# Attention and gated MLP on one core: two staging places for the sums of the u weights, their stores at set places of SyncE's order, and four copies one product later

## The chip, the core and the metric

The kernel runs as one program on one core of a Trainium2 chip. The core has a matrix engine (TensorE, PE in the profile; its weight loads are PEld), a vector engine (VectorE, DVE), a scalar engine (ScalarE, ACT), a general engine (GpSimd, POOL) and a sequencer that issues nearly all DMAs (SyncE, SP). The metric is the device time of one execution in microseconds. Before the change it is 650.03 us, the median of 3 runs (650.01 to 650.95).

## What is computed

Eight batches, twelve heads, 448 positions, head size 64; sigmoid attention and behind it a gated MLP with a product over positions:

```python
scores = scale * np.matmul(q, k.transpose(0, 1, 3, 2)) - np.log(S)
attn = 1.0 / (1.0 + np.exp(-scores))
x = np.matmul(attn, v)                      # heads side by side: 448 x 768
h = np.maximum(x @ w_in, 0.0)               # 768 x 1024
u, v = h[..., :512], h[..., 512:]
v_n = (v - mean(v)) / np.sqrt(var(v) + 1e-06)
v_s = np.einsum('ts,bsd->btd', w_spatial, v_n) + b_spatial[None, :, None]
out = (u * v_s) @ w_out                     # 512 x 768
```

All in float32. The kernel gets there by splitting an operand into a high and a low part and adding three matrix products (high by high, low by high, high by low).

## The kernel before

The batches go in four rounds `m` of two. A round has its attention, then the gate (`gate_values`, `spatial`), the u product, and the output product (`outputs`). Two-by-two blocks of the u and of the output product are formed with seven block products instead of eight (Strassen's way, in Winograd's form): for this, sums of operands and sums of weights are needed, called S1 to S4 beside the plain blocks A11, A12, A22. In the first round the u product is done straight (`gated`), and while it and the output product run, GpSimd forms the sums of the u weights that the later rounds use. They go to DRAM (`tu_dram`) and are read back in each later round (`factor_loads`).

**The weight sums** are a Python generator, `u_sums` (L589 to L613). For each of three row blocks `c`: two additions (`wsum`, L598) put high and low parts together, four subtractions (L603) form four sums, and each sum is split again into a high part (a copy, L607) and a low part (a subtraction, L609). Three of the four go to DRAM by a store on SyncE's queue (L613), the fourth stays in place of the weights it came from. There is one staging place, `other`; the second sum is staged in its own place in `w_u_s`, and the fourth is written there once that store has landed. The generator stands still at each `yield`, and each call of `load_weights(1)` moves it to the next. These calls stand all over `outputs` (once after each of many products) and in `pair` (once after each score tile and once after the value products), so the calls decide where in the program a store comes to stand.

**The order of each engine is the order of the program text**: `in_program_order` chains the instructions of every engine. So whatever stands behind a waiting store on SyncE's queue waits too. All DMAs of this part of the program stand on that one queue.

**Attention of a later round** (`attention`) is one generator that starts inside `outputs` of the round before (`between`) and runs on behind it. It goes over six pairs of units `p` (a unit is a batch and two heads). A pair has 36 score products (`psc`, L327), sigmoids on ScalarE (`at`, L335) and 24 value products (`pav`, L361); between the two come the splits of the next pair's inputs on VectorE (`qks` from `raw`, L113 and L114). The loads run ahead: `raw` (keys and queries of a unit, four places), `v` (three places), the weights `w_v` of the gate, one piece per pair (L1023), and at the end `last` (L970), the short key tiles of each pair, in the places of `raw`. Behind the first five pairs come the short scores of three pairs (L315, 24 products of half size on `last`), their value products, the same for the other three pairs, and the sixth pair.

**The output product of the first round**: `px` is formed for three column blocks by A11, copied by ScalarE to `us` (L807), then continued in the same PSUM place by A12, which therefore waits for the copy. Beside it `second_sums(i)` forms and splits the operand sums of the second half of the rows: step i stands behind the copy of block i (L774 to L787; high parts by ScalarE, low parts by `lower`, L738, on VectorE).

Of the kernel before, what the change touches and what calls it, by code (L numbers as in the profile page):

```python
# [35 lines left out]
def attn_gmlp_kernel(  # L36
# [552 lines left out]
    def u_sums():  # L589

        copy, add, sub = nc.gpsimd.tensor_copy, nc.gpsimd.tensor_add, nc.gpsimd.tensor_sub
        half = F // 2
        other = const.tile([P, 2, half], F32R, name="other")
        for c in range(NH):
            vals = []
            for cc in (2 * c, 2 * c + 1):
                val = work.tile([P, 512], F32, tag="wval", name=f"wsum_{cc}", bufs=2)
                add(val, w_u_s[:, cc, 0].bitcast(F32), w_u_s[:, cc, 1].bitcast(F32))  # L598
                vals += [val[:, :half], val[:, half:]]
                yield  # L600
            w11, w12, w21, w22 = vals
            for a, b, to in ((w12, w11, w11), (w12, w22, w12), (w22, w11, w22), (w21, w22, w21)):
                sub(to, a, b)  # L603
                yield
            own = w_u_s[:, 2 * c, :, half:]
            for k, val, stage in ((1, w11, other), (2, w12, own), (0, w22, other), (None, w21, own)):
                copy(stage[:, 0], val)  # L607
                yield
                sub(stage[:, 1], val, stage[:, 0].bitcast(F32))  # L609
                yield  # L610
                if k is not None:
                    yield
                    nc.sync.dma_start(tu_dram[:, k, c], stage.bitcast(F32))  # L613

    def u_step(ps, m, i, operand, name, start):

# [112 lines left out]
    def outputs(m, between):  # L729
# [38 lines left out]
        def second_sums(i):  # L768

            a, b = g1  # L770
            s2 = c_tile(1)[:, 1]
            three, last, two, outer = place(0, 5), place(1, 0), place(1, 1), place(1, 2, 2)
            if i == 0:
                sub(b[:, 0], b[:, 0], a[:, 0])  # L774
                add(s2, b[:, 1], b[:, 0])
                copy(three[:, 0], b[:, 0])
                copy(last[:, 0], b[:, 1])
            elif i == 1:
                add(a[:, 0], s2, a[:, 0])
                sub(a[:, 1], a[:, 1], s2)  # L780
                copy(two[:, 0], s2)
                lower(three[:, 1], b[:, 0], three[:, 0])
                lower(last[:, 1], b[:, 1], last[:, 0])
            else:
                copy(outer[:, 0], a)
                lower(two[:, 1], s2, two[:, 0])
                lower(outer[:, 1], a, outer[:, 0])  # L787
                operands[S3, 1], operands[A22, 1], operands[S2, 1] = map(halves, (three, last, two))
                operands[S1, 1], operands[S4, 1] = (halves(outer[:, :, i]) for i in range(2))

        if m:
            first, second = sums_of[m]
            hooks = ((), (), (second, second), (), (), (second,), (first,), (), (second,))
            work_of = iter([lambda gs=gs: [next(g, None) for g in gs] for gs in hooks])
        else:
            gated(b1, pairs[0])
            first_sums()
            gated(b1, pairs[1])
            work_of = iter([lambda i=i: second_sums(i) for i in range(NE)])

        def sums_work():
            next(work_of, lambda: None)()
# [2 lines left out]
        for i in range(NE):  # L805
            step(px[i], m, i, A11, 11, True)
            copy(us[i][:, 0], px[i])  # L807
            sums_work()
        for i in range(NE):
            step(px[i], m, i, A12, 21, False)  # L810
            copy(c_tile(i)[:, 0], px[i])
            nc.sync.dma_start(out[b0, i], cs[i][:, 0])
            sums_work()
        if m == 0:
            between()
        pwy = [banks(f"pw_{m}_{i}") for i in range(NE)]
        pw, py = ([t[:, j, :S] for t in pwy] for j in range(2))
        for i in range(NE):
            step(pw[i], m, i, S3, 3, True)
            load_weights(1)  # L820
            add(us[i][:, 1], us[i][:, 0], pw[i])
            sums_work()
        for i in range(NE):
            step(pw[i], m, i, A22, 4, False)
            load_weights(1)
        if m:
            between()
        for i in range(NE):
            step(py[i], m, i, S2, 2, True)
            load_weights(1)  # L830
            add(cs[i][:, 1], us[i][:, 0], py[i])
            add(cs[i][:, 1], cs[i][:, 1], pw[i])
            nc.sync.dma_start(out[b1, i], cs[i][:, 1])
        for i in range(NE):
            step(py[i], m, i, S1, 1, False)
            load_weights(1)
            add(us[i][:, 1], us[i][:, 1], py[i])
            nc.sync.dma_start(out[b1, NE + i], us[i][:, 1])
        between()
        for i in range(NE):  # L840
            step(py[i], m, i, S4, 22, False)
            load_weights(1)
            add(us[i][:, 0], us[i][:, 0], py[i])
            nc.sync.dma_start(out[b0, NE + i], us[i][:, 0])
        rest = [t for t in (*tmp, *big) if t not in (*us_tags, *cs_tags)]
        tags = [*taken, *cs_tags, *us_tags, *rest]
        taken.clear()
# [93 lines left out]
    def attention(m):  # L941
# [55 lines left out]
        def pair(p):  # L997
            full, tags = [], []
            for t in (*FIRST, *SECOND):
                full.append((*unit(p), t, attention_scores(*unit(p), t, None, free)))  # L1000
                tags.append(free.pop())
                load_weights(1)
            nc.scalar.copy(mark, full[-1][-1][:1, 0, :1])
            if p + 1 < NHP:
                splits(2 * p + 2, 2 * p + 3)
# [176 lines left out]
```

## Time and profile before

| | us |
|---|---|
| time, median of 3 runs | 650.03 |
| the profiled execution, its own time | 650.33 |
| its span on the core | 648.5 |
| TensorE busy in the span | 640.0 |
| VectorE busy | 444.3 |
| ScalarE busy | 326.6 |
| GpSimd busy | 57.6 |
| mean granted TensorE clock, share of full | 0.997 |

The span is the time from the first to the last instruction of one execution; the profiled execution took 1.8 us more than its span, and 0.30 us more than the median of the three runs. A busy TensorE is one with a matmul in flight. The granted clock is the share of full speed (2.4 GHz) that the chip let TensorE have; 0.50 is the lower level of 1.2 GHz.

### The profile page before, as it was taken

The page shows a single profiled execution, that of the slowest core. Times are in us where ns is not written, and L with a number is a line of the kernel's source. Part 1 is how long each engine was busy: PE and PEld are TensorE (multiplying, and loading weights), DVE is VectorE, ACT ScalarE, POOL GpSimd, SP SyncE. Part 2 cuts the span into 40 slices and gives each one's busy share as a digit, 9 for nine tenths or more (in the row PEclk, how much of TensorE's full clock was granted, in tenths as well). Part 3 has the DMA queues.
Part 4 walks back from the last instruction along what each step waited for, and adds up shares of the span by engine and source line. Part 5 has one row for each costly group of instructions (what it writes and reads, how often), then busy time and mean ns, then how long its engine had stood idle before and what let it go on. Part 6 is the DMA issues. An engine that isn't in the chain of part 4 may idle for free.

```text
span 648.5 us, 9489 instructions
## 1 busy us (share of the span) xinstructions
PE 640.0 (99%) x3734; PEld 488.1 (75%) x3734; DVE 444.3 (69%) x630; ACT 326.6 (50%) x519; POOL 57.6 (9%) x78
## 2 busy tenths in 40 slices
PE   9999999999999899999999999999999999999997
PEld 5555789998755368999975547899996545889997
DVE  6888779996657588445854488735775548864494
ACT  5888384223366448611436674930317655681040
POOL 0000011150638001000000000000000000010000
PEclk9999999999999899999999999999999999999999
DMA  8864732073887600543176830047038690032313
GB/s 307 260 228 147 277 96 65 2 297 129 307 280 218 211 2 1 196 162 156 59 262 232 249 130 1 11 184 286 33 129 283 206 293 22 0 130 104 109 43 127
DMA packets 40748, 101.01 MB, mean 156 GB/s; under 512 B 8448, under 2 KB 22528, under 8 KB 40448
## 3 DMA queue, kind: packets, MB, share of 16 engines
q1 hardware_dynamic: 40704, 100.42, 44.6%
q8 instruction: 29, 0.48, 0.3%
q14 instruction: 15, 0.12, 0.1%
HBM read 80.74 MB, written 19.66 MB: 155 GB/s over the span
## 4 chain that ended last, share of the span: by engine, by line
PE 70%; issue 13%; DVE 9%; DMA 4%; POOL 2%; ACT 1%; SPq 1%; POOLq 0%; DVEq 0%; ACTq 0%
PE pv L380 13%; PE pav L361 12%; PE pw L380 11%; PE psc L327 8%; PE pg L380 8%; PE ux L380 7%; PE uy L380 5%; PE px L380 4%; DMA last<-qk_dram 2%; PE psc L315 1%; DMA tu_dram<-w_u_s 1%; DVE vn L431 1%; DVE wval L149 1%; DVE wval L146 1%; DMA tu_dram<-other 1%
## 5 line engine op out<-in xcount | busy, mean ns | idle before, releaser
L335 ACT ACTIVATE at<-psc,bias_s 128x896 f32<-128x896 f32 x168 | 155.6, 1015 | 106.0 <-PE psc L327 81.8
L361 PE MATMUL pav<-at,v 128*64 128x448 f32 (+1 forms) x624 | 119.1, 543 | 0.0
L380 PE MATMUL pv<-w_v,x_s 128*128 128x512 f32 x504 | 115.5, 390 | 0.0
L380 PEld LDWEIGHTS pv<-w_v,x_s 128*128 128x128 f32 x504 | 94.3, 188 | 22.3 <-issue 2.8
L327 PEld LDWEIGHTS psc<-qks 64*128 64x128 f32 x864 | 79.4, 185 | 21.4 <-issue 13.6
L327 PE MATMUL psc<-qks 64*128 64x448 f32 x864 | 94.2, 367 | 0.0
L361 PEld LDWEIGHTS pav<-at,v 128*64 128x64 f32 (+1 forms) x624 | 40.9, 136 | 66.1 <-issue 46.2
L380 PE MATMUL pg<-w_sp_s,vn 128*128 128x448 f32 x352 | 71.7, 362 | 0.0
L380 PEld LDWEIGHTS pg<-w_sp_s,vn 128*128 128x128 f32 x352 | 66.0, 188 | 4.6
L984 DVE COPY whole<-pav 128x896 f32<-128x896 f32 x15 | 16.4, 1092 | 59.4 <-PE pav L361 55.3
L114 DVE TENSOR_TENSOR qks<-raw,qks 128x848 fp32r<-128x848 f32 (+2 forms) x48 | 51.6, 1082 | 6.4 <-ACT qks L113 5.3
L380 PE MATMUL pw<-x_s,factors 128*128 128x448 f32 x261 | 53.8, 362 | 0.0
L380 PEld LDWEIGHTS pw<-x_s,factors 128*128 128x128 f32 x261 | 48.9, 187 | 3.3
L415 POOL TENSOR_SCALAR rstd<-power 128x2 f32<-128x2 f32 (+1 forms) x16 | 4.0, 249 | 461.9 <-ACT pv L412 461.9
L431 DVE SCALAR_TENSOR_TENSOR vn<-rv,rstd,vn 128x512 fp32r<-128x512 f32 (+1 forms) x32 | 23.3, 748 | 23.5 <-ACT vn L426 23.3
L380 PE MATMUL ux<-x_s,w_u_s 128*128 128x448 f32 x162 | 33.4, 362 | 0.0
L426 ACT ACTIVATE vn<-rv,rstd 128x512 fp32r<-128x512 f32 (+1 forms) x32 | 21.8, 717 | 20.7 <-POOL rstd L416 20.6
L380 PEld LDWEIGHTS ux<-x_s,w_u_s 128*128 128x128 f32 x162 | 30.4, 187 | 2.1
L989 DVE TENSOR_TENSOR whole<-whole,pav 128x896 f32<-128x896 f32 x18 | 18.9, 1084 | 15.4 <-PE pav L361 15.4
L380 PE MATMUL pu<-x_s,w_u_s 128*128 128x448 f32 x144 | 29.1, 362 | 0.0
L380 PEld LDWEIGHTS pu<-x_s,w_u_s 128*128 128x128 f32 x144 | 27.0, 187 | 1.8
L656 ACT CAST x_s<-g 128x896 fp32r<-128x896 f32 x6 | 5.6, 941 | 42.9 <-DVE g L649 42.9
(150 smaller groups left out, 812.5 us busy)
## 6 DMA issues: line engine op xcount, KB each, us to landing
raw<-qk_dram SPq DMA_DIRECT2D x47, 456.0 KB, 5.6
v<-v_dram SPq DMA_DIRECT2D x23, 448.0 KB, 5.2
w_v<-w_v_dram SPq DMA_DIRECT2D x18, 512.0 KB, 5.4
factors<-t_dram SPq DMA_DIRECT2D x12, 768.0 KB, 4.8
last<-qk_dram SPq DMA_DIRECT2D x18, 448.0 KB, 5.2
factors<-tu_dram SPq DMA_DIRECT2D x9, 768.0 KB, 5.8
wraw<-w_in_dram SPq DMA_DIRECT2D x12, 512.0 KB, 6.9
out_dram<-cs SPq DMA_DIRECT2D x24, 224.0 KB, 1.9
```

Of the source, the lines that this page charges most:

```text
L114: nc.vector.tensor_sub(lo, src, hi.bitcast(F32))
L146: nc.vector.scalar_tensor_tensor(l, a, 3, l, op0=ALU.logical_shift_left, op1=ALU.bitwise_or)
L149: nc.vector.scalar_tensor_tensor(l, low, 29, l, op0=ALU.logical_shift_right, op1=ALU.bitwise_or)
L315: nc.tensor.matmul(psc[odd * HALF : (odd + 1) * HALF, j, :S], key[rows], query[rows], start=True, stop=True,)
L327: nc.tensor.matmul(psc[:, j, :S], s[rows, a, k : k + P], s[rows, e, REST:PART], start=i == 0, stop=i == len(TERMS) - 1,)
L335: nc.scalar.activation(at, psc[:, :, :S], AF.Sigmoid, bias=bias_s, scale=QK)
L361: nc.tensor.matmul(pav[heads, odd, :S], vt[rows, heads], at[rows, j], start=start, stop=stop)
L380: nc.tensor.matmul(ps, st, mv, start=start and i == 0, stop=i == len(ops) - 1, skip_group_check=not start)
L426: nc.scalar.mul(hi, rv[rows, i], rstd[rows, i : i + 1])
L431: nc.vector.scalar_tensor_tensor(lo, rv[rows, i], rstd[rows, i : i + 1], hi.bitcast(F32), op0=ALU.mult, op1=ALU.subtract,)
L984: copy(whole, pav)
L989: nc.vector.tensor_add(whole, whole, pav)
```

## The change

`u_sums` has two staging places, `others[0]` and `others[1]`, used in turn. A step `stage(n)` forms and splits one sum; the sum that stays in place is now written first of its row block, straight from the additions, and nothing is staged in `w_u_s`. Each move of the generator issues store `n` and then works on sum `n + 2`. The calls of `load_weights` are taken out of the loops and stand at chosen places: one behind the first product of `outputs`, two behind the second, one behind each of the last three, and two in each `pair` (one behind all score tiles, one behind the value products). `second_sums` has four steps instead of three: its copies and lower parts move one step, that is one product, later.

```diff
-        other = const.tile([P, 2, half], F32R, name="other")
-        for c in range(NH):
...
-            own = w_u_s[:, 2 * c, :, half:]
-            for k, val, stage in ((1, w11, other), (2, w12, own), (0, w22, other), (None, w21, own)):
-                copy(stage[:, 0], val)
-                yield
-                sub(stage[:, 1], val, stage[:, 0].bitcast(F32))
-                yield
-                if k is not None:
-                    yield
-                    nc.sync.dma_start(tu_dram[:, k, c], stage.bitcast(F32))
+        others = [const.tile([P, 2, half], F32R, name=f"other_{i}") for i in range(2)]
+
+        def halved(to, val):
+            copy(to[:, 0], val)
+            sub(to[:, 1], val, to[:, 0].bitcast(F32))
+
+        def stage(n, vals):
+            if n % 3 == 0:
...
+                w11, w12, w21, w22 = vals
+                for a, b, to in ((w12, w11, w11), (w12, w22, w12), (w22, w11, w22), (w21, w22, w21)):
+                    sub(to, a, b)
+                halved(w_u_s[:, 2 * c, :, half:], w21)
+            halved(others[n % 2], vals[(0, 1, 3)[n % 3]])
+
+        vals = []
+        stage(0, vals)
+        stage(1, vals)
+        for n in range(3 * NH):
+            yield
+            nc.sync.dma_start(tu_dram[:, (1, 2, 0)[n % 3], n // 3], others[n % 2].bitcast(F32))
+            if n + 2 < 3 * NH:
+                stage(n + 2, vals)
@@ second_sums(i) in outputs
             if i == 0:
                 sub(b[:, 0], b[:, 0], a[:, 0])
                 add(s2, b[:, 1], b[:, 0])
-                copy(three[:, 0], b[:, 0])
-                copy(last[:, 0], b[:, 1])
             elif i == 1:
                 add(a[:, 0], s2, a[:, 0])
                 sub(a[:, 1], a[:, 1], s2)
+                copy(three[:, 0], b[:, 0])
+                copy(last[:, 0], b[:, 1])
+            elif i == 2:
                 copy(two[:, 0], s2)
+                copy(outer[:, 0], a)
                 lower(three[:, 1], b[:, 0], three[:, 0])
                 lower(last[:, 1], b[:, 1], last[:, 0])
             else:
-                copy(outer[:, 0], a)
                 lower(two[:, 1], s2, two[:, 0])
                 lower(outer[:, 1], a, outer[:, 0])
@@ outputs: calls of load_weights
+        load_weights(1)
         for i in range(NE):
             step(px[i], m, i, A12, 21, False)
             copy(c_tile(i)[:, 0], px[i])
             nc.sync.dma_start(out[b0, i], cs[i][:, 0])
             sums_work()
+        load_weights(2)
...
@@ pair(p) in attention
             for t in (*FIRST, *SECOND):
                 full.append((*unit(p), t, attention_scores(*unit(p), t, None, free)))
                 tags.append(free.pop())
-                load_weights(1)
+            load_weights(1)
```

ScalarE in the first round's output product, before. `x_s` are the high parts of the operand sums, `us` the copies that free the three `px` places for A12:

```order
L759 CAST x_s_76<-g_0_0_1099 128x2x448
L760 CAST x_s_76<-cs_0_0_1355 128x448
L807 COPY us_0_0_1314<-px_0_0_1404 128x448
L776 CAST x_s_76<-g_1_2_1299 128x448
L777 CAST x_s_76<-g_1_2_1299 128x448
L807 COPY us_0_1_1315<-px_0_1_1405 128x448
L781 CAST x_s_76<-cs_0_1_1414 128x448
L807 COPY us_0_2_1316<-px_0_2_1406 128x448
L785 CAST x_s_76<-g_0_2_1139 128x2x448
```

The same stretch of ScalarE after the change:

```order
L766 CAST x_s_76<-g_0_0_1099 128x2x448
L767 CAST x_s_76<-cs_0_0_1355 128x448
L815 COPY us_0_0_1314<-px_0_0_1404 128x448
L815 COPY us_0_1_1315<-px_0_1_1405 128x448
L786 CAST x_s_76<-g_1_2_1299 128x448
L787 CAST x_s_76<-g_1_2_1299 128x448
L815 COPY us_0_2_1316<-px_0_2_1406 128x448
L789 CAST x_s_76<-cs_0_1_1414 128x448
L790 CAST x_s_76<-g_0_2_1139 128x2x448
```

The second `us` copy now stands ahead of the two casts of `g_1_2`, and the third ahead of the cast of `cs_0_1`. VectorE's order is the same before and after.

SyncE's queue from the first loads behind the first round's outputs, before (`raw_3_0` is the unit of batch 3, heads 0 and 1; the stores are those to `tu_dram`; two of nine stand ahead of this stretch):

```order
L271 DMA v_2_4_1611<-v_dram 128x896
L613 DMA tu_dram_82<-other_1478 128x512
L262 DMA raw_3_0_1699<-qk_dram 128x912
L262 DMA raw_3_1_1701<-qk_dram 128x912
L271 DMA v_3_0_1703<-v_dram 128x896
L1023 DMA w_v_1_1606<-w_v_dram_78 128x1024
L613 DMA tu_dram_82<-other_1478 128x512
L262 DMA raw_3_2_1788<-qk_dram 128x912
L262 DMA raw_3_3_1790<-qk_dram 128x912
```

The same stretch after the change, with five stores ahead of it:

```order
L271 DMA v_2_4_1645<-v_dram 128x896
L618 DMA tu_dram_82<-other_1_1440 128x512
L618 DMA tu_dram_82<-other_0_1439 128x512
L262 DMA raw_3_0_1729<-qk_dram 128x912
L262 DMA raw_3_1_1731<-qk_dram 128x912
L271 DMA v_3_0_1733<-v_dram 128x896
L1031 DMA w_v_1_1640<-w_v_dram_78 128x1024
L618 DMA tu_dram_82<-other_1_1440 128x512
L618 DMA tu_dram_82<-other_0_1439 128x512
L262 DMA raw_3_2_1814<-qk_dram 128x912
L262 DMA raw_3_3_1816<-qk_dram 128x912
```

Here stand the sixth to ninth store, all of them ahead of `raw_3_2`, where there were the third and the fourth.

SyncE's queue at the end of the fifth pair, before (`last_2_4` and `last_3_0` are the short key tiles of the third and the fourth pair):

```order
L1023 DMA w_v_1_1606<-w_v_dram_78 128x1024
L613 DMA tu_dram_82<-other_1478 128x512
L613 DMA tu_dram_82<-w_u_s_79 128x2x256
L613 DMA tu_dram_82<-other_1478 128x512
L970 DMA last_2_4_2065<-qk_dram 128x2x64
L970 DMA last_2_4_2065<-qk_dram 128x2x448
L970 DMA last_3_0_2068<-qk_dram 128x2x64
L970 DMA last_3_0_2068<-qk_dram 128x2x448
```

The same place after the change:

```order
L1031 DMA w_v_1_1640<-w_v_dram_78 128x1024
L978 DMA last_2_4_2067<-qk_dram 128x2x64
L978 DMA last_2_4_2067<-qk_dram 128x2x448
L978 DMA last_3_0_2070<-qk_dram 128x2x64
L978 DMA last_3_0_2070<-qk_dram 128x2x448
```

The last three stores, which stood ahead of these loads, are gone from here.

## Rows read from the trace of the kernel before

**Rows 1.** The page's first section: busy time, share and instructions of each engine.

```profile
PE 640.0 (99%) x3734; PEld 488.1 (75%) x3734; DVE 444.3 (69%) x630; ACT 326.6 (50%) x519; POOL 57.6 (9%) x78
```

**Rows 2.** Busy time by stretch: length, then PE, PEld, DVE, ACT, POOL, clock, DMA.

```profile
140.00:150.00 10.00, 9.02 (x45) 8.12 (x44) 9.83 (x14) 5.81 (x11) 1.08 (x2) 1.00 0.87 319
...
210.00:220.00 10.00, 6.86 (x52) 2.58 (x52) 3.17 (x3) 2.91 (x3) 1.57 (x3) 0.84 0.87 272
```

**Rows 3.** Timeline of PE at px: start, us, operation, [idle before, releaser].

```profile
141.60 4.97 PE L380 MATMUL px<-gs,w_out_s 128*128 128x448 f32 x24
147.54 2.68 PE L380 MATMUL px<-gs,w_out_s 128*128 128x448 f32 x12 [0.98 <-ACT us L807]
150.06 14.56 PE L380 MATMUL pw<-x_s,factors 128*128 128x448 f32 x72
```

**Rows 4.** The chain that ended last: the same px products in the second round.

```profile
305.17 7.21 PE px L380 x36
```

**Rows 5.** Timeline of ACT in the stretch of rows 3.

```profile
146.03 0.57 ACT L776 CAST x_s<-g 128x448 fp32r<-128x448 f32 x1 [2.46 <-DVE g L774]
...
146.97 0.52 ACT L807 COPY us<-px 128x448 f32<-128x448 f32 x1
```

**Rows 6.** Timeline of DVE in the same stretch.

```profile
138.77 1.05 DVE L756 TENSOR_TENSOR cs<-g 128x448 f32<-128x448 f32 x1
...
141.57 2.23 DVE L738 TENSOR_TENSOR x_s<-g,x_s 128x896 fp32r<-128x896 f32 x2
...
145.37 0.62 DVE L774 TENSOR_TENSOR g<-g,g 128x448 f32<-128x448 f32 x1
```

**Rows 7.** Timeline of PE: fourth pair, short scores, sixth pair, in the second round's attention.

```profile
193.60 3.88 PE L327 MATMUL psc<-qks 64*128 64x448 f32 x36
...
210.54 1.73 PE L315 MATMUL psc<-last 64*64 64x448 f32 x16
215.42 0.98 PE L315 MATMUL psc<-last 64*64 64x448 f32 x8 [3.14 <-DMA last<-qk_dram]
...
224.99 3.88 PE L327 MATMUL psc<-qks 64*128 64x448 f32 x36
```

**Rows 8.** Timeline of PE: short scores and sixth pair, third and fourth round.

```profile
372.67 2.49 PE L315 MATMUL psc<-last 64*64 64x448 f32 x24
...
382.21 3.88 PE L327 MATMUL psc<-qks 64*128 64x448 f32 x36
...
529.88 2.49 PE L315 MATMUL psc<-last 64*64 64x448 f32 x24
...
539.73 3.88 PE L327 MATMUL psc<-qks 64*128 64x448 f32 x36
```

**Rows 9.** Busy time by stretch, as rows 2, one microsecond behind the wait.

```profile
217.00:218.00 1.00, 1.00 (x11) 0.42 (x7) 0.49 (x1) 0.53 (x1) 0.00 (x0) 0.50 1.07 359
```

**Rows 10.** Timeline of SP in the second round's attention.

```profile
171.33 1.72 SPq L262 DMA_DIRECT2D raw<-qk_dram  x2
...
210.52 0.32 SPq L613 DMA_DIRECT2D tu_dram<-other  x1
210.93 1.96 SPq L970 DMA_DIRECT2D last<-qk_dram  x4
```

**Rows 11.** Timeline of SP in the third round's attention, same loads.

```profile
367.09 2.47 SPq L970 DMA_DIRECT2D last<-qk_dram  x4
```

**Rows 12.** Timeline of POOL: the third store's sum, and the second row block.

```profile
164.99 0.40 POOL L607 CAST other<-wsum 128x256 fp32r<-128x256 f32 x1 [23.82 <-DMA tu_dram<-other]
...
171.75 3.31 POOL L598 TENSOR_TENSOR wsum<-w_u_s 128x512 f32<-128x512 f32 x2
...
181.20 1.41 POOL L609 TENSOR_TENSOR w_u_s<-wsum,w_u_s 128x256 fp32r<-128x256 f32 x1
```

**Rows 13.** DMA issues from 180 to 195 us: size of one, median us to landing.

```profile
raw<-qk_dram SPq DMA_DIRECT2D x4, 456.0 KB, 6.1
```

**Rows 14.** Busy time by stretch, as rows 2; its end is DMA share and GB/s.

```profile
174.00:180.00 6.00, 6.00 (x50) 3.92 (x48) 3.19 (x4) 3.25 (x5) 5.68 (x7) 1.00 0.96 357
```

More of the change, by code (lines that the diff above doesn't have):

```diff
@@ L592, in u_sums @@
         half = F // 2
-        other = const.tile([P, 2, half], F32R, name="other")
-        for c in range(NH):
[L595 to L599, printed above, removed]
-                yield
-            w11, w12, w21, w22 = vals
-            for a, b, to in ((w12, w11, w11), (w12, w22, w12), (w22, w11, w22), (w21, w22, w21)):
-                sub(to, a, b)
-                yield
-            own = w_u_s[:, 2 * c, :, half:]
-            for k, val, stage in ((1, w11, other), (2, w12, own), (0, w22, other), (None, w21, own)):
-                copy(stage[:, 0], val)
-                yield
-                sub(stage[:, 1], val, stage[:, 0].bitcast(F32))
-                yield
-                if k is not None:
-                    yield
-                    nc.sync.dma_start(tu_dram[:, k, c], stage.bitcast(F32))
+        others = [const.tile([P, 2, half], F32R, name=f"other_{i}") for i in range(2)]
[4 more added lines that the diff above has]
+            if n % 3 == 0:
+                c = n // 3
+                vals.clear()
+                for cc in (2 * c, 2 * c + 1):
+                    val = work.tile([P, 512], F32, tag="wval", name=f"wsum_{cc}", bufs=2)
+                    add(val, w_u_s[:, cc, 0].bitcast(F32), w_u_s[:, cc, 1].bitcast(F32))
+                    vals += [val[:, :half], val[:, half:]]
+                w11, w12, w21, w22 = vals
[11 more added lines that the diff above has]
+                stage(n + 2, vals)
     def u_step(ps, m, i, operand, name, start):
@@ L798, in outputs @@
             gated(b1, pairs[1])
-            work_of = iter([lambda i=i: second_sums(i) for i in range(NE)])
+            work_of = iter([lambda i=i: second_sums(i) for i in range(NE + 1)])
         def sums_work():
@@ L833, in outputs @@
             nc.sync.dma_start(out[b1, i], cs[i][:, 1])
+        load_weights(1)
         for i in range(NE):
             step(py[i], m, i, S1, 1, False)
-            load_weights(1)
             add(us[i][:, 1], us[i][:, 1], py[i])
             nc.sync.dma_start(out[b1, NE + i], us[i][:, 1])
+        load_weights(1)
         between()
@@ L841, in outputs @@
             step(py[i], m, i, S4, 22, False)
-            load_weights(1)
             add(us[i][:, 0], us[i][:, 0], py[i])
             nc.sync.dma_start(out[b0, NE + i], us[i][:, 0])
+        load_weights(1)
         rest = [t for t in (*tmp, *big) if t not in (*us_tags, *cs_tags)]
@@ L1001, in pair @@
                 tags.append(free.pop())
-                load_weights(1)
+            load_weights(1)
             nc.scalar.copy(mark, full[-1][-1][:1, 0, :1])
```

2 lines of the change are left out of this document (removed).

## The prediction

> **What bounds the kernel now.** I read the page's busy times first: TensorE is busy for 640.0 of 648.5 us [rows 1], so an edit on another engine is worth only what TensorE now stands idle, or runs slow, because of it. The table by stretch then shows where that is. Two stretches stand out in the part of the program that the diff touches: 140 to 150, with 9.02 us busy of 10, and 210 to 220, with 6.86 of 10 and a mean clock of 0.84 [rows 2]. The timeline of TensorE names the releasers. At 146.6 it waits 0.98 us for a `us` copy of ScalarE [rows 3]. At 212.3 it waits 3.14 us for a `last` load [rows 7]. Behind that second wait the granted clock is 0.50, the 1.2 GHz level [rows 9]; a mean of 0.84 over 10 us makes that about (1 - 0.84) x 10 / 0.5 = 3.2 us long [rows 2]. Around the first wait it stayed at 1.00 [rows 2].
>
> An idle figure leaves out the drain of the products before it and the slow ones behind it, so I price both places by a start-to-start distance against the same work in another round.
>
> First place: 36 `px` products run from 141.60 to 150.06, 8.46 us [rows 3]; in the second round they take 7.21 [rows 4]. It costs 1.25.
>
> Second place: from the start of the short scores to the sixth pair, 224.99 - 210.54 = 14.45 us [rows 7]; in the third round 382.21 - 372.67 = 9.54, in the fourth 539.73 - 529.88 = 9.85 [rows 8]. It costs 4.60 to 4.91, of which 3.14 is the wait and up to 1.77 the lower clock and the refill.
>
> The later rounds run the same loads without any weight sums, so they are what the second round should look like with the stores out of the way.
>
> **The copies, one product later.** Nothing is added or removed; ScalarE's order changes. Before, the second `us` copy stands behind two casts of `g_1_2`, which wait for VectorE's L774 until 146.03; the copy ends at 146.97 + 0.52 = 147.49 and TensorE goes on at 147.54 [rows 3, 5]. Its source, the second `px` block, is complete after 12 products of 0.2 us, at 144.0. After, that copy runs at 144.0 to 144.5, far ahead of its use. The third copy now takes the second's slot and ends at 147.49. It is wanted by the 31st product, at 141.60 + 30 x 0.2 = 147.6, whose weights are loaded one product earlier, 147.4. So the wait does not vanish by a wide margin: what is late next is this third copy, by 0.1 to 0.15. Gain 1.25 - 0.15 = 1.1, if VectorE's chain to L774 stays where it is.
>
> It may not stay. GpSimd's work moves: six operations that split sums (the sum left in `w_u_s`, then both staging places) come where four were before the generator stopped, and they last about 2.5 us longer into this stretch, to some 143.7. VectorE's L756 beside GpSimd took 1.05, where L774 of the same size, with GpSimd standing still, took 0.62 [rows 6]: 0.43 per hit. The two lower parts L738 at 141.57 are newly beside GpSimd. On the other side the first write now waits for the last read of the plain weights by TensorE, which leaves L754 and L756 alone for a while. I take 0.1 net and keep from no hit (gain 1.25) to two hits behind a late copy (1.25 - 0.15 - 0.86 = 0.24). Taken: **1.0**.
>
> The Trainium skill (SBUF — State Buffer, section Who interferes with whom) speaks against this part: it says that a VectorE instruction with two SBUF inputs and a GpSimd instruction that reads SBUF do not share the port, one is blocked for the whole instruction. By that rule a hit would cost up to a GpSimd subtraction, 1.41 us as in [rows 12], the whole gain of the copies would go, and the time would be 645.4; the row's 0.43 is less than that, so here the trace does not bear it out in full, and the sum goes by the row.
>
> Behind `px` nothing waits for the moved lower parts: VectorE's order is unchanged, and the first operand that `pw` needs of them is cast at the same 146.03.
>
> **The stores.** Nine stores, and GpSimd's 42 operations, are the same in number. Before, one staging place and a late first store made GpSimd idle 23.82 us for that store [rows 12], so the sums ran late and the last store was issued at 210.52, with the `last` loads of the third and fourth pair right behind it at 210.93 [rows 10]. In the third round the same loads are issued at 367.09, 5.58 us ahead of the short scores [rows 8, 11]; here they were issued 0.39 us behind their start. After, no store stands there, all four calls in `pair` being used up in the second pair. What bounds these loads next is the split that frees their places and the transfers ahead of them, as in the third and fourth round. That gives 4.91 by the third round and 4.60 by the fourth, which still waited a little for `last`. I take **4.6**, since here the queue has been held up more than in either.
>
> What pays for it is the queue in the first two pairs. The seventh store stands ahead of `raw_3_0` and waits for the first sum of the third row block. GpSimd can begin that block when it has used the landing of the fourth store. The fourth store stands where the second stood before, and the work on that landing ended at 171.75 [rows 12]; 1.0 earlier now, 170.75. The second row block took from 171.75 to 181.20 + 1.41 = 182.61, 10.86 us for the same ten operations [rows 12]. So the seventh store goes at about 181.6 and `raw_3_0` at 182.0, where it went at 171.33 before [rows 10]. At 6.1 us to landing [rows 13] it is there at 188.1. Its products begin at 193.60 - 1.0 = 192.6 [rows 7], and between lie two VectorE operations of at most 1.1 each (L738 of 896 columns: 2.23 for two [rows 6]). TensorE is covered by 2.3 us. The ninth store waits for the seventh to land and one more split, and `raw_3_2` behind it is wanted one pair later, 8.5 us ((210.54 - 193.60) / 2 [rows 7]). So the delay costs nothing by this count; without that cover every microsecond of it would be TensorE's.
>
> VectorE's operations of the last three products read one operand from PSUM. GpSimd's second row block now lies beside them; I bound that by the hit above, 0 to 0.43 each. They only empty PSUM places that TensorE wants again one product of three blocks later, and I take 0.
>
> **The sum.** Profiled execution 650.33 - 1.0 - 4.6 = 644.7. The median of the runs was 0.30 lower: 650.03 - 5.6 = **644.4**. With all terms at their ends: 650.03 - 1.25 - 4.91 = 643.9 to 650.03 - 0.24 - 4.60 = 645.2. Everything behind the sixth pair shifts as a whole, since TensorE is without a pause there.
>
> **Rivals.**
>
> (a) *The gap at the short scores shrinks but stays.* The loads that `raw_3_0` heads are issued 10.7 us late and must catch up. At 357 GB/s, the rate of a stretch with the engines 0.96 busy [rows 14], a load of 456 KB takes 1.3 us. If two of them are still queued when the last `last` loads go, these land 2.6 us late, and the fourth round shows that they have no slack. Then 644.4 + 2.6 = 647.0, and with the lower clock behind it again 648.8. For it: the late queue. Against it: the loads behind have 20 us to catch up in, and DMA stood idle in part of them before. Chance 0.20, spread over 645.2 to 648.7.
>
> The page TensorE: Matmul & The Clock Gate of the Trainium skill (What's actually happening) says that the gate judges on a grid of its own that does not begin with the program. By that rule even a shorter gap could be answered by the lower clock, and 648.8 would be the time of this rival rather than 647.0; the trace has one wait with it and one without [rows 2, 9], which fits but does not decide.
>
> (b) *The gap stays whole*, because the loads are bound by the splits here and not by the stores: only the copies gain, 650.03 - 1.0 = 649.0. Against it: SyncE's rows, with the store 0.4 us ahead of the load [rows 10]. Chance 0.06.
>
> (c) *Slower: the queue blocks the fourth pair.* Place: seventh store, `raw_3_0`. It decides from 192.6 - 2.2 - 6.1 - 0.4 = 183.9: a first sum ready later than that makes TensorE wait as much. To end over 1.3 us slower it must eat 5.6 + 1.3, of which a second fall of the clock would give 1.8, so 5.1 of waiting: a sum at 189.0, 7.4 us later than worked out, for work that took 10.9 before. 650.03 + 1.3 and more, say 652. For it: GpSimd slowed by VectorE, whose splits now fall beside it. Chance 0.06.
>
> (d) *The change does not do what it says for the copies* (VectorE late by more than two hits): 645.4. It lies at the edge of the forecast and is counted with (a).
>
> **How the numbers follow.** Forecast 644.4, 643.9 to 645.2: 0.65. (a) and (d) 0.20, (b) 0.06, (c) 0.06, better than the forecast's ends 0.03. The range 643.7 to 647.2 holds the forecast, most of the better case and two thirds of (a), 0.8. A measurement of this kernel can tell about 0.2%, 1.3 us, from no change. Faster by more than that (under 648.7): forecast, better, and (a), 0.87. Within: (b), and a little of (a) and (c), 0.08. Slower: 0.05.
>
> **What would show it.** Right: 36 `px` products in 7.2 to 7.6 us; short scores to sixth pair in 9.5 to 9.9, with the clock at 1.00; no store to `tu_dram` later than about 190; `raw_3_0` issued near 182 and the fourth pair of the second round still following the third without a pause. Wrong: a wait of TensorE for `raw` or `qks` between 185 and 205, a wait for `last` of more than 0.5 us, or VectorE's L774 later than 146.4.

## The result

The changed kernel took 643.64 us (median of 4 runs, 643.47 to 644.28) against 650.49 for the kernel before (4 runs, 650.01 to 653.01): ratio 0.9889, 95% interval 0.9862 to 0.9916. Two later series, each on one chip with its own runs of before, gave 644.14 against 650.82 (0.9898, 0.9882 to 0.9915) and 643.93 against 650.60 (0.9893, 0.9876 to 0.9911). It is faster by 1.0 to 1.1%, 6.7 to 6.9 us, where 5.6 was forecast. One execution among all that follow ran at a mean granted clock of 0.85 (712 us, in the run called late_block); it is left out.

Both waits of TensorE that the prediction priced are gone. The table by stretch of the changed kernel (length, then busy time of PE, PEld, DVE, ACT, POOL, the granted clock, DMA share and GB/s) answers [rows 2]:

```profile
140.00:150.00 10.00, 10.00 (x51) 9.06 (x50) 9.68 (x13) 7.13 (x13) 4.10 (x4) 1.00 0.76 302
...
210.00:220.00 10.00, 10.00 (x104) 4.14 (x98) 7.90 (x10) 6.98 (x8) 0.00 (x0) 1.00 0.50 177
```

Before, TensorE was busy for 9.02 and 6.86 us in these two stretches. TensorE's timeline in the changed kernel answers [rows 3, 7, 8] (start, us, line, operation; an idle time ahead of a row would stand in brackets):

```profile
140.74 7.61 PE L380 MATMUL px<-gs,w_out_s 128*128 128x448 f32 x36
148.18 14.79 PE L380 MATMUL pw<-x_s,factors 128*128 128x448 f32 x72
162.82 3.77 PE L380 MATMUL pw<-x_s,w_out_s 128*128 128x448 f32 x18
166.51 3.88 PE L327 MATMUL psc<-qks 64*128 64x448 f32 x36
...
208.90 2.49 PE L315 MATMUL psc<-last 64*64 64x448 f32 x24
...
218.44 3.88 PE L327 MATMUL psc<-qks 64*128 64x448 f32 x36
```

No row has an idle time. `px` takes 148.18 - 140.74 = 7.44 us, where it took 8.46; short scores to sixth pair take 218.44 - 208.90 = 9.54, where they took 14.45 and where the third round always took 9.54. SyncE's queue shows the stores at work, answering [rows 10]:

```profile
169.96 11.14 SPq L618 DMA_DIRECT2D tu_dram<-other  x2
181.20 0.88 SPq L262 DMA_DIRECT2D raw<-qk_dram  x2
...
183.12 1.33 SPq L618 DMA_DIRECT2D tu_dram<-other  x2
...
203.32 2.47 SPq L978 DMA_DIRECT2D last<-qk_dram  x4
```

The sixth and seventh store hold the queue for 11.14 us, and `raw_3_0` follows at 181.20 (182.0 was forecast). The last store is issued by 184.45 instead of 210.52. The `last` loads of the third and fourth pair go at 203.32, 5.58 us ahead of the short scores, the very distance of the third round.

From start to end, the two profiled executions differ like this (start-to-start distances in TensorE's timeline, us):

| stretch | before | after | difference |
|---|---|---|---|
| start of the program to `px` of the first round | 141.60 | 140.74 | -0.86 |
| `px` | 8.46 | 7.44 | -1.02 |
| `pw` of the first round to the first pair | 18.10 | 18.33 | +0.23 |
| five pairs | 42.38 | 42.39 | +0.01 |
| short scores to sixth pair, second round | 14.45 | 9.54 | -4.91 |
| from there to the fourth round's short scores | 304.89 | 304.90 | +0.01 |
| short scores to sixth pair, fourth round | 9.85 | 9.54 | -0.31 |
| from there to the end of the span | 108.77 | 108.82 | +0.05 |

The sum is -6.80, and the spans are 648.5 and 641.7. The 0.86 of the first line is there by the first gate product, at 66 us, ahead of everything that the change moves.

### The profile page after: what moved, and what is told of

Same layout as the page of the kernel before. It is cut to its first block, busy times and chain, and to the rows that moved or that the text cites. A ratio compares the mean times of both kernels' runs of the same rounds, so it can differ in the third digit from the quotient of the medians.

```text
span 641.7 us, 9491 instructions
## 1 busy us (share of the span) xinstructions
PE 637.5 (99%) x3734; PEld 486.3 (76%) x3734; DVE 441.5 (69%) x630; ACT 326.5 (51%) x519; POOL 56.0 (9%) x78
## 4 chain that ended last, share of the span: by engine, by line
PE 99%; DVE 0%; issue 0%
PE pav L361 20%; PE pv L380 18%; PE psc L327 14%; PE pw L380 11%; PE pg L380 11%; PE ux L380 7%; PE uy L380 5%; PE px L380 5%; PE pu L380 4%; PE psc L315 3%; PE idle L1081 1%; DVE us L850 0%
## 5 line engine op out<-in xcount | busy, mean ns | idle before, releaser
L114 DVE TENSOR_TENSOR qks<-raw,qks 128x848 fp32r<-128x848 f32 (+2 forms) x48 | 50.1, 1050 | 5.7 <-ACT qks L113 4.5
```

What stands on the lines that cost most here:

```text
L114: nc.vector.tensor_sub(lo, src, hi.bitcast(F32))
```

## The experiments

The theory: two independent waits, one on ScalarE's copies and one on late stores, and the 0.86 at the start is spread. The rivals: the start belongs to the change; the copies' gain is eaten at the later wait; the stores gain by their places alone, or by the second staging place alone.

### Both kernels once more: before_again, after_again, after_third

> The kernel before, once more, for the spread of its start. In the first two profiles the whole program after the change runs 0.86 us early at its 72nd u product, ahead of anything that the change touches: the second unit's first load landed later in the run of before (VectorE waits for it until 7.00, against 6.16). My theory: that is spread between executions, so this profile may show the first pair's value products (PE, pav) begin anywhere from 9.3 to 10.3 us; the two waits (0.98 at px, 3.1 at the short scores with the low clock behind it) stand as before. Rival: the 0.86 belongs to the change, then all profiles of before begin them at about 10.2. Time: 650.0 to 651.

> The changed kernel, once more. By my theory its value products begin anywhere from 9.3 to 10.3 us, px takes 7.4 us, short scores to sixth pair 9.5 us in all three later rounds or up to 0.3 more in one. By the rival they begin at 9.4 always. Time: 643.5 to 644.3, a ratio of 0.989 to 0.991 against before.

> The changed kernel beside the run above, for a comparison on one chip: 643.5 to 644.6, with px at 7.4 and pw to attention at 18.33.

before_again took 651.34 us (12 runs, 649.59 to 652.88), no different from before (ratio 1.0004, 0.9991 to 1.0017); after_again 644.14 (643.60 to 644.61), after_third 643.93 (643.50 to 644.70). The place where 0.86 us came in at the start is VectorE's wait for the second unit's keys and queries. VectorE's timeline before, and then after the change:

```profile
7.00 0.47 DVE L113 CAST qks<-raw 128x592 fp32r<-128x592 f32 x1 [1.99 <-DMA raw<-qk_dram]
```

```profile
6.16 0.47 DVE L113 CAST qks<-raw 128x592 fp32r<-128x592 f32 x1 [1.10 <-DMA raw<-qk_dram]
```

The first gate product (`pv`) began at 66.49 and 66.47 in the two profiles of before, at 65.64, 65.84 and 65.70 in the three of after. By these five alone the rival would stand. The other kernels speak against it: it began at 65.64 in copies_only and 65.69 in two_places_old_calls, which have the stores' places of before, and at 66.36 in stores_only, 66.05 in stores_behind_loads, 66.36 in one_place_new_calls and 66.62 in late_block_2, which have the changed ones. So both kinds have both ends, and neither part of the change carries the start with it.

That it varies between executions of one kernel, and is not set once for each built kernel, is not shown by the profiles: the two of before differ by 0.02, the three of the changed kernel by 0.20. The times lean to it. From stores_only to after_again the profiles give 1.22 at `px` less 0.23 behind it, 0.99, and 0.52 more at the start; the medians of their executions differ by 0.99, without the 0.52.

before_again showed something else. Its wait for `last` was longer, and the low clock behind it too (TensorE's timeline, and the table by stretch for 210 to 220):

```profile
210.53 1.74 PE L315 MATMUL psc<-last 64*64 64x448 f32 x16
216.22 1.77 PE L315 MATMUL psc<-last 64*64 64x448 f32 x8 [3.95 <-DMA last<-qk_dram]
217.74 4.36 PE L361 MATMUL pav<-at,last_v 64*64 64x448 f32 x24
...
226.74 3.47 PE L327 MATMUL psc<-qks 64*128 64x448 f32 x32
```

```profile
210.00:220.00 10.00, 6.05 (x41) 1.97 (x41) 1.54 (x2) 2.91 (x3) 2.20 (x4) 0.74 0.75 236
```

Here the short scores cost 226.74 - 210.53 = 16.21 us, 1.76 more than in the execution that the prediction was made from, at a mean clock of 0.74 instead of 0.84. What differs is how long the seventh store took to land: the ninth sum goes to the same staging place and waits for it. SyncE's and GpSimd's rows in the first profile of before, and then in before_again:

```profile
204.49 0.33 SPq L613 DMA_DIRECT2D tu_dram<-other  x1
...
209.29 0.40 POOL L607 CAST other<-wsum 128x256 fp32r<-128x256 f32 x1 [2.61 <-DMA tu_dram<-other]
```

```profile
203.09 0.38 SPq L613 DMA_DIRECT2D tu_dram<-other  x1
...
210.06 0.40 POOL L607 CAST other<-wsum 128x256 fp32r<-128x256 f32 x1 [7.17 <-DMA tu_dram<-other]
```

In before_again the seventh store was issued 1.40 us earlier, but its place came free 6.97 us behind the issue instead of 4.80, and the last store went at 211.30 instead of 210.52. In the series beside these runs the kernel before ran 23 times, from 648.50 to 652.54, with a mean granted clock of 1.000 in 2 of them, 0.999 in 1, 0.997 in 15 and 0.995 in 5; the five at 0.995 are at 651.56 to 652.54. A mean of 0.995 over some 649 us is about (1 - 0.995) x 649 / 0.5 = 6.5 us at the lower level, 0.997 about 3.9; the means are given to 0.001, which is 1.3 us. The changed kernel ran at 0.999 or 1.000 each time (14 runs in three series), and within 1.2 us.

### Each part alone: copies_only, stores_only

> The kernel before with the four steps of second_sums alone; weight sums and their calls as before. If the parts are independent: px 36 products in 7.2 to 7.5 us instead of 8.46, the short scores still 14.4 us, time 1.0 us less than before. GpSimd does not run on beside VectorE here, so px may come out up to 0.2 shorter than in the full change. Rival (the gain of the copies is eaten at the short scores, since the last loads stay where they are in time and TensorE only waits longer for them): the short scores take 15.4 us and the time is that of before.

> The changed kernel with second_sums as before. Independent parts: short scores to sixth pair 9.5 us, no store later than 185, px at 8.5 to 9.2 (GpSimd now beside VectorE), time 644.6 to 645.6, that is 4.5 to 5.5 less than before. Rival: the stores alone hold the queue and some of the wait stays, 646 or more.

The edit of copies_only is the `second_sums` part of the diff on the kernel before; that of stores_only is all the rest.

stores_only took 645.13 us (644.79 to 645.53), ratio 0.9913 (0.9899 to 0.9928) against 650.82: 5.7 us less. Against after_again beside it, 644.14, the copies are worth 1.0 there, the small loss behind `px` included. Its profile has all three short-score stretches at 9.53 or 9.54 and `px` at 8.63. This one came out as expected.

copies_only took 649.63 (12 runs, 648.84 to 651.68), ratio 0.9989 with an interval of 0.9976 to 1.0002: 1.2 less, but not separable from no change among executions that spread over 3 us. Its `px` took 7.29 us; its short scores 15.64, with a wait of 4.33 (TensorE's timeline):

```profile
214.82 0.98 PE L315 MATMUL psc<-last 64*64 64x448 f32 x8 [4.33 <-DMA last<-qk_dram]
```

The rival says that this wait is longer because TensorE came there earlier and the last loads did not. SyncE's queue lends it no support: the seventh store was issued at 201.31, 7.45 us ahead of the short scores, as in before_again (7.44), and its place came free 7.23 us later, at 208.54 (6.97 there). So the stores came earlier with TensorE, and the longer wait lies with the landing, which varies without the copies too:

```profile
201.31 0.38 SPq L613 DMA_DIRECT2D tu_dram<-other  x1
...
208.54 0.40 POOL L607 CAST other<-wsum 128x256 fp32r<-128x256 f32 x1 [5.86 <-DMA tu_dram<-other]
```

One profile and times within noise leave open whether a part of the copies' gain is eaten as long as the later wait stands; it is not eaten in the full change.

### One half of the stores' part alone: two_places_old_calls, one_place_new_calls

> The kernel before with a second staging place (the first three sums of a row block go to the two places in turn, the fourth stays in place), all calls and so all stores where they stood on SyncE's queue. Theory A (a store late because its sum is late holds the last loads): GpSimd still waits 23 us for the first store, but gains some 3 us at the second and 11 at the fifth, so the last store goes at about 207 instead of 210.5 and the last loads behind it just in time: short scores to sixth pair 9.6 to 11 us, time 3.5 to 4.9 less than before. Theory B (the place on the queue costs, whatever the sum's time): 14 us stay, time as before.

```diff
-        other = const.tile([P, 2, half], F32R, name="other")
+        others = [const.tile([P, 2, half], F32R, name=f"other_{i}") for i in range(2)]
+        staged = 0
...
-            for k, val, stage in ((1, w11, other), (2, w12, own), (0, w22, other), (None, w21, own)):
+            for k, val in ((1, w11), (2, w12), (0, w22), (None, w21)):
+                stage = own if k is None else others[staged % 2]
+                staged += 1 if k is not None else 0
```

It took 649.54 (8 runs) against 651.24 in its series: 1.7 us less, ratio 0.9978 (0.9965 to 0.9991). I expected 3.5 to 4.9. Its short scores took 13.61 us, and GpSimd's and SyncE's timelines say why:

```profile
208.06 0.40 POOL L610 CAST other<-wsum 128x256 fp32r<-128x256 f32 x1 [9.32 <-DMA tu_dram<-other]
```

```profile
202.34 7.28 SPq L616 DMA_DIRECT2D tu_dram<-other  x3
209.71 1.96 SPq L973 DMA_DIRECT2D last<-qk_dram  x4
```

The last three stores stand in a row at 202.34, and with two places the ninth sum cannot be formed before the seventh store has landed, which was so in the kernel before too. GpSimd had stood idle 9.32 us, all sums ahead of that one done, when the landing came at 208.06, 5.7 us behind the issue. I had the last store at 207; it went at 209.6. So neither theory holds alone: the sums are early, but the place still makes the `last` loads wait for a landing. The profiled execution is the fastest of the eight.

> The changed kernel with one staging place instead of two: each sum is formed once the store before it has been issued, the stores at the changed places. The sum then waits for the landing of the store right before it. By my count the seventh store goes at about 187.7 instead of 181.2 and the ninth near 198, both ahead of raw loads: TensorE waits about 3.5 us in the fourth pair and 2 more in the fifth, with a lower clock behind: 649 to 653, at or above before. Rival (the places alone carry the gain): 644.

```diff
-            halved(others[n % 2], vals[(0, 1, 3)[n % 3]])
+            halved(other, vals[(0, 1, 3)[n % 3]])
...
-        stage(1, vals)
...
-            if n + 2 < 3 * NH:
-                stage(n + 2, vals)
+            if n + 1 < 3 * NH:
+                stage(n + 1, vals)
```

It took 649.72 (10 runs) against 651.24: 1.5 us less, ratio 0.9976 (0.9960 to 0.9991), in the range expected. This kernel has the copies one product later too (its `px` takes 7.26 us), so about 1.0 of the 1.5 is theirs. The queue was held twice (SyncE's timeline):

```profile
174.31 10.38 SPq L617 DMA_DIRECT2D tu_dram<-other  x2
184.78 0.88 SPq L262 DMA_DIRECT2D raw<-qk_dram  x2
...
187.88 8.11 SPq L617 DMA_DIRECT2D tu_dram<-other  x2
196.08 0.89 SPq L262 DMA_DIRECT2D raw<-qk_dram  x2
...
208.64 2.34 SPq L977 DMA_DIRECT2D last<-qk_dram  x4
```

But the waits were not where I put them. The five pairs lost only 1.3 us (43.65 for 42.38); the rest came out at the short scores, 15.72 us in the profiled execution, the slowest of the ten. The loads issued late reach the `last` loads on the same queue: those of the third and fourth pair went 2.08 us ahead of the short scores, at 210.72, instead of 5.58:

```profile
215.74 1.77 PE L315 MATMUL psc<-last 64*64 64x448 f32 x8 [2.70 <-DMA last<-qk_dram]
```

So the stores' places alone are worth about 0.5 us (1.5 less the copies' 1.0, an estimate that takes the two as independent), the second staging place alone 1.7, and both together 5.7 (stores_only): either half leaves a store that waits for a landing ahead of loads that TensorE needs, only at another place.

### What the held queue costs: stores_behind_loads, late_block, late_block_2

> The changed kernel with the seventh and ninth store moved behind the raw, v and w_v loads of their pair, so that these loads no longer wait 11 us on the queue. By my count the wait is covered (raw of the fourth pair landed over 4 us ahead of need): time that of the changed kernel within 0.2. Rival: the late loads cost something by crowding the DMA engines: 0.3 us or more faster.

```diff
             if p + 1 < NHP:
-                load_weights(1)
                 copy_sums(p, pav, copy)
...
             weight_loads(p)
+            load_weights(1)
```

It took 644.25 us, ratio 0.9889 (0.9874 to 0.9904), beside 0.9889 to 0.9898 of the changed kernel: the same. The times could not show 0.3 us, but the distances agree: five pairs in 42.39 us and short scores in 9.54, as in the changed kernel. The 11 us on the queue are covered, as worked out. (Its profile has a wait of 0.85 for `last` in the fourth round, like the 0.28 and 0.91 of before.)

> The changed kernel with the two additions of the third row block done three times, four extra operations of about 1.75 us on GpSimd: the seventh store goes 7 us later, near 188. My count: raw of the fourth pair lands near 193, its split ends near 194.8, and TensorE, which wants it at 192.0, waits 2.5 to 3.5 us; with a lower clock behind the wait 1.5 us more: 3 to 5 us slower than the changed kernel. If there is more cover than I counted: less than 1 us.

> The kernel of late_block once more, since the profile of its first run came from an execution in which the whole chip ran at a clock of 0.85. Its other three runs took 647.1 to 648.0, 3.0 to 3.9 above the changed kernel. Expected in the profile: seventh store near 188, a wait of TensorE for the splits of the fourth pair (start between 192 and 197) of 2 to 3.5 us, with the clock falling behind it in some runs; if instead the pause is at the short scores, the late loads had caught up too little there.

```diff
-                    add(val, w_u_s[:, cc, 0].bitcast(F32), w_u_s[:, cc, 1].bitcast(F32))
+                    for _ in range(3 if c == 2 else 1):
+                        add(val, w_u_s[:, cc, 0].bitcast(F32), w_u_s[:, cc, 1].bitcast(F32))
```

The second series gave 647.98 us (8 runs, 647.38 to 649.08), 4.0 above after_third beside it; the remaining runs of the first were 647.08 to 648.02. The size is as expected, the place again only in part. SyncE's row and TensorE's timeline of late_block_2:

```profile
171.13 16.71 SPq L619 DMA_DIRECT2D tu_dram<-other  x2
```

```profile
193.58 1.88 PE L327 MATMUL psc<-qks 64*128 64x448 f32 x16 [0.18 <-DVE qks L114]
196.16 2.08 PE L327 MATMUL psc<-qks 64*128 64x448 f32 x18 [0.70 <-DVE whole L993]
...
214.65 0.98 PE L315 MATMUL psc<-last 64*64 64x448 f32 x8 [1.61 <-DMA last<-qk_dram]
...
220.04 0.98 PE L315 MATMUL psc<-last 64*64 64x448 f32 x8 [0.34 <-DMA last<-qk_dram]
```

With `raw_3_0` behind the seventh store at 187.94 instead of 181.20, 5.8 us later counted from `px` (which came 0.98 later here), the fourth pair is touched by a few tenths at each of two places (1.45 in the five pairs), and 11.90 - 9.54 = 2.36 are lost at the short scores, where the first wait ends 27 us behind that late load. In the stretches of these waits the clock stayed at 1.00. The profiled execution, the slowest of the eight, also lost 0.93 in the fourth round, at a wait for `last` of 0.92.

### The two small losses that were left: both_waits_less

> The changed kernel with the two small losses taken out that its profile still shows in the output product of the first round. (1) px takes 7.44 us and not 7.21, since the third us copy stands behind two casts on ScalarE that wait for VectorE: the casts go one more step later, behind that copy. (2) From the first pw product to the attention 18.33 us and not 18.10, since VectorE splits the first unit's inputs ahead of the first addition that frees pw: the split goes behind the three additions. Expected from the distances: px 7.21 and pw 18.10, 0.4 to 0.5 us faster than the changed kernel. Rival: the later casts make VectorE's lower parts late for pw, which then waits; no gain or up to 0.5 lost.

The weight-load timeline of the changed kernel shows both losses, a wait for the third `us` copy and one for the first addition:

```profile
146.87 1.11 PEld L380 LDWEIGHTS px<-gs,w_out_s 128*128 128x128 f32 x6 [0.34 <-ACT us L815]
147.99 3.59 PEld L380 LDWEIGHTS pw<-x_s,factors 128*128 128x128 f32 x18
151.90 10.71 PEld L380 LDWEIGHTS pw<-x_s,factors 128*128 128x128 f32 x54 [0.33 <-DVE us L830]
```

```diff
             elif i == 1:
                 add(a[:, 0], s2, a[:, 0])
                 sub(a[:, 1], a[:, 1], s2)
-                copy(three[:, 0], b[:, 0])
-                copy(last[:, 0], b[:, 1])
             elif i == 2:
+                copy(three[:, 0], b[:, 0])
+                copy(last[:, 0], b[:, 1])
...
         load_weights(2)
-        if m == 0:
-            between()
...
             add(us[i][:, 1], us[i][:, 0], pw[i])
             sums_work()
+        if m == 0:
+            between()
```

Its timeline:

```profile
140.77 7.36 PE L380 MATMUL px<-gs,w_out_s 128*128 128x448 f32 x36
147.97 14.56 PE L380 MATMUL pw<-x_s,factors 128*128 128x448 f32 x72
162.37 3.77 PE L380 MATMUL pw<-x_s,w_out_s 128*128 128x448 f32 x18
166.06 3.88 PE L327 MATMUL psc<-qks 64*128 64x448 f32 x36
```

`px` is at 7.20 (7.43 in after_third) and `pw` at 18.09 (18.34): 0.48 us gained in the profile, as expected. The times, 643.59 (643.05 to 644.92) against 643.93, differ by 0.34; five runs each, spread over 1.9 and 1.2 us, do not tell that from no change. It is the version I would keep, on the strength of the distances.

## Why the prediction missed

The mechanism held step by step; the size was short, and the range ended at 643.7, 0.06 above the first series of four. The later two series, 644.14 and 643.93, lie inside it; that does not mend it, since the gain over the runs of before beside them is 6.7, where its lower end allowed for 6.3. On which side of 643.7 a series came was luck: the three differ by 0.5 among themselves. That the gain was larger than the range allowed for was not.

**The copies.** Right in size: 1.0 forecast, 1.02 at `px` in the profiles. The 1.0 between stores_only and after_again is 1.19 to 1.22 at `px` less the 0.23 behind it. The third copy came out as the next late thing and VectorE as the second part: with the copies alone, where GpSimd does not run on, `px` takes 7.29, 0.08 above the 7.21 of the second round, and in the full change 0.15 more. VectorE's timeline, answering [rows 6]:

```profile
137.71 0.63 DVE L763 TENSOR_TENSOR cs<-g 128x448 f32<-128x448 f32 x1
...
140.08 2.83 DVE L745 TENSOR_TENSOR x_s<-g,x_s 128x896 fp32r<-128x896 f32 x2
...
144.69 0.63 DVE L781 TENSOR_TENSOR g<-g,g 128x448 f32<-128x448 f32 x1
```

The addition that had taken 1.05 beside GpSimd takes 0.63, and the two lower parts take 2.83 instead of 2.23, GpSimd now being beside them. L781 (L774 before) begins 3.95 us behind the first `px` product instead of 3.77: 0.18 net, where I took 0.1. The Trainium skill (SBUF — State Buffer, Who interferes with whom) says that one of the two is blocked for the whole instruction. The prediction put the price of a hit by that rule at 1.41 us, and found that the trace bears it out only in part. But such a GpSimd subtraction takes 0.74 undisturbed; the rest of the 1.41 is its own wait. GpSimd's timeline, and VectorE's second operation of the two at 140.08:

```profile
140.49 1.47 POOL L597 TENSOR_TENSOR other<-wsum,other 128x256 fp32r<-128x256 f32 x1
...
183.37 0.74 POOL L597 TENSOR_TENSOR other<-wsum,other 128x256 fp32r<-128x256 f32 x1
```

```profile
141.29 1.63 DVE L745 TENSOR_TENSOR x_s<-g,x_s 128x896 fp32r<-128x896 f32 x1
```

The subtraction is listed from 140.49 but ends at 141.96, 0.67 after VectorE's first operation gave way to the second at 141.29: about its own undisturbed length. VectorE's second operation ends at 142.92, 0.96 behind the subtraction, where two such take 2.23 undisturbed. So each seems to have waited for the other to end, and here the trace agrees with that rule; by it the price of such a hit is at most GpSimd's own 0.74, not 1.41.

**Behind `px`.** A miss of 0.23: I wrote that nothing waits there. VectorE splits the first unit's inputs (L114) ahead of the additions that free `pw`, before and after the change. VectorE's rows before, and then after:

```profile
151.68 1.04 DVE L114 TENSOR_TENSOR qks<-raw,qks 128x848 fp32r<-128x848 f32 x1 [1.22 <-ACT qks L113]
152.64 1.84 DVE L821 TENSOR_TENSOR us<-us,pw 128x448 f32<-128x448 f32 x3
```

```profile
150.27 1.04 DVE L114 TENSOR_TENSOR qks<-raw,qks 128x848 fp32r<-128x848 f32 x1 [0.49 <-ACT qks L113]
151.23 1.68 DVE L830 TENSOR_TENSOR us<-us,pw 128x448 f32<-128x448 f32 x3
```

That chain came 1.41 us earlier, `pw` 1.88 (148.18 instead of 150.06). So the first addition starts 3.05 us behind the first `pw` product instead of 2.58, and TensorE meets an addition that had been done in time before. copies_only has the loss too (18.34 for 18.10), and both_waits_less shows the cause by taking it away. The mistake was to check the moved operands and not VectorE's next operation against the earlier TensorE.

**The stores.** This is the step that failed: the term was taken as 4.6, with 4.91 as its far end. The profile pair gives 4.91, and the comparison of times 5.7 (stores_only against before). I read the price of the wait from one execution and its bounds from undisturbed rounds, so both bounds were on the side of what replaces it, and none on the side of what is removed. The two profiles of before have 14.45 and 16.21 us at that place, that is 4.91 and 6.67 above 9.54. The wait follows the landing of the seventh store (4.80 and 6.97 us behind its issue), with a low clock behind it, and so it varies between executions; of the three runs before (650.01, 650.03, 650.95) two, and the profiled one (650.33), lay in the lower half of what the kernel does (650.82 in the middle of 23 runs, 648.5 to 652.5).

A second part of it: I took the fourth round's 9.85 as the model because the queue is held up in the second. That extra 0.31 was itself a wait of that kind (0.28 in this profile, 0.91 in before_again, none in three profiles of the changed kernel, 0.85 in stores_behind_loads); the third round's 9.54 was the better model, and the wait's absence in the fourth round gave another 0.31 in this pair of profiles.

**What covered the held queue.** Right: `raw_3_0` issued 0.8 us ahead of the time worked out, no wait in the fourth pair, and stores_behind_loads gains nothing. I had the cover at 2.3 us, too small: the load is split from 184.88, 3.7 us behind its issue, not 6.1, and the DMA engines were only 0.43 busy from 170 to 180. late_block_2, 5.8 us later, is about where it ends for the fourth pair.

**The rivals.** (a) did not come, but it is what a later queue does: in late_block_2 and one_place_new_calls the loss comes out mainly at the short scores, as (a) had it, and not in the pair that (c) named. (b) and (d) fell with the first profile. (c) would have needed more than the 5.8 us of late_block_2, which is still faster than before by 2.6.

**The clock.** The page TensorE: Matmul & The Clock Gate of the Trainium skill (What's actually happening) says that the gate judges on a grid of its own. The runs agree as far as they go: the length of a wait does not settle whether the clock falls. Waits of 2.57, 0.77 and 0.39 us in two_places_old_calls were followed by 1.00 throughout (the mean of that execution is 1.000), those of 0.36 and 2.70 in one_place_new_calls by a fall, and 3.14 and 3.95 in the kernel before cost 3.2 and at least 5.2 us at the lower level. That a grid is the reason no run here shows. The table by stretch for two_places_old_calls, and then for one_place_new_calls:

```profile
209.00:219.00 10.00, 6.66 (x66) 2.40 (x66) 4.20 (x5) 3.72 (x4) 1.35 (x3) 1.00 0.86 277
```

```profile
209.00:219.00 10.00, 6.95 (x46) 2.28 (x46) 1.09 (x1) 3.02 (x3) 0.00 (x0) 0.78 1.06 393
```

Six of the eight executions of two_places_old_calls had a mean clock of 0.997, so there too it fell in some. I named this for a gap that stays, and did not apply it to the gap that goes: its price is a spread as well.

## What to carry to other kernels

When a wait that is removed ends in a transfer, and a fall of the clock can follow it, its price in one profile is one draw: take the spread of the runs of before into the lower end of the range too. A store that waits for its data on a queue shared with loads costs where the loads run out of cover, which can be far behind it; early data and a place that does not need a landing have to come together, as here one half gave 1.7 and the other about 0.5 of 5.7 us. And when TensorE is moved earlier, check the next operation of every engine that frees its places, not only the operations that the change moves.

## What the runs showed that was not expected

The kernel with the wait varies more than the one without: 12 runs of before_again spread over 3.3 us, 5 of after_again over 1.0, on the same chip (5 of both_waits_less, on another, over 1.9). Two more places differ from profile to profile, whatever the stores: the first 10 us, where the landing of the first loads moves the whole program by up to 1.0 us, and the short scores of the fourth round, where 4 of the 12 profiles (late_block's aside) have a wait for `last` of 0.28 to 0.92 us. Whether these two make up the rest of the spread was not tested.
